# Keeping a threshold chain and a score's input in PSUM, with a second Y pair and a two-multiplication negation on POOL

## The chip, the core and the metric

The kernel runs on one core of a Trainium2 chip. The core has five engines with a queue each: TensorE (PE, whose weight loads are shown as PEld), VectorE (DVE), ScalarE (ACT), GpSimd (POOL) and SyncE (SP, which here only issues DMAs). Each queue runs in order; the engines meet through semaphores. Matmuls write PSUM, which PE, DVE and ACT reach and POOL and the DMAs do not; everything else lies in SBUF. The metric is the device time of one execution in microseconds (us), median of several runs; less is better.

## What is computed

The input x has 8 batches of 3136 rows of 256 numbers. The first half is a layer in the frequency domain with a soft threshold, the second sends 128 rows of each batch through a small network:

```python
X = np.fft.rfft(x, axis=1)
Yr = Xr @ w_r - Xi @ w_i + b_r
Yi = Xr @ w_i + Xi @ w_r + b_i
Y* = np.sign(Y*) * np.maximum(np.abs(Y*) - lam, 0.0)        # lam = 0.01, for Yr and Yi
x = np.fft.irfft(Yr + 1j * Yi, n=3136, axis=1)
scores = np.einsum('bsd,d->bs', x, w_gate)
# per batch: the 128 rows with the largest scores
h = np.maximum(x[top] @ w1, 0.0)
out[top] = x[top] + sigmoid(scores[top])[:, None] * (h @ w2)   # other rows: out = x
```

## The kernel before

The transform of length 3136 is done as 98 x 32 with matmuls. Per batch there are five stages. s1 multiplies by the 98-point table, 16 pieces of 98 x 512, and its result goes through HBM (scratch As). s2 does the 32-point half for 13 pieces g (12 of two frequency groups, one of one) into the PSUM tile px. spectral multiplies by the complex weights into the PSUM tile py, thresholds, and leaves the pair Yh, Yl. s2i does the inverse 32-point half into a PSUM tile named s, copies it to ct, takes the scalar product with w_gate for the scores, and writes ct to HBM (scratch Cs). s1i does the inverse 98-point half and writes the output. So that fp32 keeps its precision at a fast matmul format, most operands are split into a high part (a cast on ACT) and a low part (source minus high part, on DVE or POOL), and every product is three matmuls (mm3, lines 221 to 223).

One loop of about 140 steps drives all of it. In step t it emits s1 of a piece 16 steps ahead, s2 of piece t+1, spectral of piece t, s2i of piece t-1, and s1i of a piece 17 steps back; 104 steps have a spectral piece. Threads of the routing half (select, place, gather, the network) are ticked along between them; their small matmuls use the PSUM tile m. The queues are not written by hand: a scheduler that keeps the program's priorities, its pools of buffers and its own estimates of durations decides the order on each engine. A pool hands a buffer out again when the last reader of its former content is done, so a change of what reads a buffer changes waits as well.

PSUM has eight banks and all are used: four for s (s1, s2i and s1i take turns), one for px, two for py, one for m.

The lines that matter here. In spectral, line 438 adds the bias plus 0.01 to py and writes v in SBUF (DVE); line 440 makes r1 = relu(v - 0.02) on ACT; line 441 makes r1 = min(v, 0) + r1 (DVE), which is the soft threshold; line 442 splits r1 by lines 215 (Yh, ACT) and 217 (Yl = r1 - Yh, DVE). The profile names r1 as r. There is one pair Yh, Yl (YB = 1). In s2i, line 459 copies s to ct (ACT) and line 462, twice, multiplies ct by wgb and sums (DVE; the page calls it CUSTOM_DVE_ANT_0 with an accumulator read behind it). In s2, lines 420 and 421 write Xh and its negated part (ACT), line 422 writes Xl (DVE) and line 423 its negated part (POOL). Line 217 also stands for POOL's two low parts xl and cl, from SBUF only. In consts_a, lines 168 to 172 load the two weights through the buffers v and split them.

Of the kernel before, what the change touches and what calls it, by code (L numbers as in the profile page):

```python
# [10 lines left out]
F32 = mybir.dt.float32  # L11
# [5 lines left out]
AF = mybir.ActivationFunctionType  # L17
ALU = mybir.AluOpType

B, S, D = 8, 3136, 256  # L20
N1, N2 = 98, 32
NJ = 25
NF = 64
# [85 lines left out]
def fourier_moe(ctx: ExitStack, tc: tile.TileContext, x, w_r, w_i, b_r, b_i, wg, w1, w2,  # L109
                t_w1, t_w1t, t_wf, t_wq, t_g, t_gi, t_m, t_dig, outs, cap):  # L110
    nc = tc.nc
# [3 lines left out]
    pool = ctx.enter_context(tc.tile_pool(name="work", bufs=2))  # L115
# [6 lines left out]
    As, Cs, xt, xs, at, ct, av, cv, cs, ot, X, Y, Csc = [{} for _ in range(13)]  # L122

    def c_tile(shape, dt, name):
        return const.tile(shape, dt, name=name)
# [9 lines left out]
    bias = c_tile([128, 2, D], F32, "bias")  # L135
    m2l = c_tile([128, 1], F32, "m2l")
# [24 lines left out]
    def ld(out, src):  # L161
        queued(nc.sync, lambda: nc.sync.dma_start(out=out, in_=src))
# [3 lines left out]

    def consts_a():
        for src, h, l in ((w_r, wrh, wrl), (w_i, wih, wil)):
            t = pool.tile([128, 2, D], F32, name="v")
            ld(t, src.rearrange("(h p) e -> p h e", p=128))  # L170
            nc.vector.tensor_copy(h, t)
            nc.vector.tensor_tensor(out=l, in0=t, in1=h.bitcast(F32), op=ALU.subtract)
        for c, src in enumerate((b_r, b_i)):
            ld(bias[c * NF:(c + 1) * NF], src.rearrange("(o a e) -> o a e", o=1, a=1).broadcast_to([NF, 2, D]))
        nc.vector.tensor_scalar(out=bias, in0=bias, scalar1=LAM, scalar2=None, op0=ALU.add)
        nc.vector.memset(m2l, -2.0 * LAM)
# [32 lines left out]
    def pair(h_shape, tag, bufs):  # L209
        return (pool.tile(h_shape, F32R, name=tag + "h", bufs=bufs),  # L210
                pool.tile(h_shape, F32R, name=tag + "l", bufs=bufs))

    def split(src, tag, bufs, sub, track={}):
        h = pool.tile(list(src.shape), F32R, name=tag + "h", bufs=bufs)
        nc.scalar.copy(out=h, in_=src)  # L215
        l = pool.tile(list(src.shape), F32R, name=tag + "l", bufs=bufs)
        track[sub] = sub.tensor_tensor(out=l, in0=src, in1=h.bitcast(F32), op=ALU.subtract).ins  # L217
        return h, l

    def mm3(out, wh, wl, mh, ml, start=True, stop=True):  # L220
        nc.tensor.matmul(out, wh, mh, start=start, stop=False)  # L221
        nc.tensor.matmul(out, wl, mh, start=False, stop=False)  # L222
        return nc.tensor.matmul(out, wh, ml, start=False, stop=stop).ins  # L223
# [140 lines left out]
    def jview(t):  # L364
        return t[:96].rearrange("(j q) n d -> j (q n) d", q=4)

    def tail_rows(t):
        return t[96:].rearrange("q n d -> (q n) d")

    def width(g):  # L370
        return 1 if g == G - 1 else 2
# [38 lines left out]
    def s2(b, g):  # L410
        a = av.pop((b, g))
        w = width(g)
        r = a.shape[0]
        px = ps.tile([128, 2 * w, 128], F32, name="px", bufs=1)
        for p in range(w):
            for h in range(2):
                nc.tensor.matmul(px[:, 2 * p + h, :], a[:, 2 * (g % 2) * (w - 1) + p, h * 128:(h + 1) * 128],  # L417
                                 g_sb[:r, 2 * g + p, :], start=True, stop=True)
        xh, xl = pair([128, 2 * w, 3 * NF], "X", 2)
        nc.scalar.copy(out=xh[:, :, NF:], in_=px)  # L420
        nc.scalar.mul(out=xh[:, :, :NF], in_=px[:, :, NF:], mul=-1.0)  # L421
        nc.vector.tensor_tensor(out=xl[:, :, NF:], in0=px, in1=xh[:, :, NF:].bitcast(F32), op=ALU.subtract)  # L422
        nc.gpsimd.tensor_scalar(out=xl[:, :, :NF], in0=xl[:, :, 2 * NF:].bitcast(F32), scalar1=-1.0, scalar2=None, op0=ALU.mult)  # L423
        X[b, g] = xh, xl

    def spectral(b, g):
        w = width(g)
        py = ps.tile([128, w, D], F32, name="py", bufs=2)
        xh, xl = X.pop((b, g))
        for p in range(w):  # L430
            k = 0
            for sl, wh, wl in ((slice(NF, 3 * NF), wrh, wrl), (slice(0, 2 * NF), wih, wil)):
                for h in range(2):
                    mm3(py[:, p, :], xh[:, 2 * p + h, sl], xl[:, 2 * p + h, sl], wh[:, h, :], wl[:, h, :],
                        start=(k == 0), stop=(k == 3))
                    k += 1
        v = pool.tile([128, w, D], F32, name="v")
        nc.vector.tensor_tensor(out=v, in0=py, in1=bias[:, :w, :], op=ALU.add)  # L438
        r1 = pool.tile([128, w, D], F32, name="r1",bufs=1)
        nc.scalar.activation(out=r1, in_=v, func=AF.Relu, bias=m2l, scale=1.0)  # L440
        nc.vector.scalar_tensor_tensor(out=r1, in0=v, scalar=0.0, in1=r1, op0=ALU.min, op1=ALU.add)  # L441
        Y[b, g] = split(r1, "Y", YB, nc.vector)

    def s2i(b, g):
        w = width(g)
        if g == 0:
            Cs[b] = dram.tile([N1, N2, D], F32, name="Cs")
            Csc[b] = pool.tile([128, NJ], F32, name="Csc")
            nc.vector.memset(Csc[b][:, NJ - 1:], 0.0)
        if g % 2 == 0:  # L450
            ct[b] = pool.tile([128, 4, D], F32, name="ct")
        yh, yl = Y.pop((b, g))
        r = 128 if w == 2 else 64
        p = ps.tile([r, w, D], F32, name="s", bufs=4)
        for q in range(w):
            mm3(p[:, q, :], gih[:, 2 * g + q, :r], gil[:, 2 * g + q, :r], yh[:, q, :], yl[:, q, :])
        o = 2 * (g % 2)
        c = ct[b][:r, o:o + w, :]
        nc.scalar.copy(out=c, in_=p)  # L459
        for k in range(w):  # L460
            junk = pool.tile([128, D], F32, name="junk", bufs=1)
            nc.vector.tensor_tensor_reduce(out=junk[:r], in0=c[:, k, :], in1=wgb[:r], scale=1.0, scalar=0.0,  # L462
                                           op0=ALU.mult, op1=ALU.add, accum_out=Csc[b][:r, 2 * g + k:2 * g + k + 1])
        if w == 1:
            nc.sync.dma_start(out=tail_rows(Cs[b]), in_=c[:, 0, :])
        elif g % 2 == 1:
            nc.sync.dma_start(out=jview(Cs[b])[2 * g - 2:2 * g + 2].rearrange("j p d -> p j d"), in_=ct[b])

# [35 lines left out]
        if i % 2 == 1:  # L504
            nc.sync.dma_start(out=ov[b][:, 2 * i - 2:2 * i + 2, :], in_=ot[b])

    HB, YB = 2, 1
    G, U = 13, 16
    main_pe = [None]
    LEAD, LAG, XP, AP = 16, 17, 4, 2  # L510
# [69 lines left out]
    for t in range(-LEAD - XP, B * G + LAG + 1):  # L580
        if t + LEAD + XP < G:
            at_step(t + LEAD + XP, ld_x, U)
        at_step(t + LEAD + 1, split_x, U)
        at_step(t - LAG + 1, split_c, U)
        at_step(t + LEAD, s1, U)
        at_step(t + AP, ld_a, G)
        if t + LEAD + XP >= G:
            at_step(t + LEAD + XP, ld_x, U)
        at_step(t - LAG + 2, ld_c, U)
        if t == -LEAD + 7:  # L590
            consts_a()
        if t % 2 == 0 and (t + 4) // 2 in range(0, 7):
            consts_g((t + 4) // 2)
        if t % 2 and (t + 1) // 2 in range(0, 7):
            consts_gi((t + 1) // 2)
        if t == 10:
            consts_b()
        if t in range(20, 20 + 2 * (FF // 128 + 2), 2):
            consts_moe((t - 20) // 2)
        at_step(t + 1, s2, G)  # L600
        tick(threads)
        at_step(t, spectral, G)
        at_step(t - 1, s2i, G, "s2i")
        tick(threads)
        at_step(t - LAG, s1i, U, "s1i")
        if main_pe[0] is not None:
            with tc.issue_after(main_pe[0]):
                tick(ffns)
# [29 lines left out]
```

## Time and profile before

| what | us |
|---|---|
| median of 3 runs (lowest, highest) | 802.58 (802.05, 802.77) |
| the profiled execution, span of its core | 802.3 |
| PE busy in it | 745.9 (93%) |
| PEld busy | 654.1 (82%) |
| DVE busy | 616.3 (77%) |
| ACT busy | 489.5 (61%) |
| POOL busy | 427.9 (53%) |

The profile shows one execution, so durations and waits come from that one; its span is within 0.3 us of the median, and no more of its time is given than the span. PE's busy share counts matmuls whose ends are modelled and overlap, so it overstates how near PE is to its own limit; the share of weight loads, of which there is one per matmul, is the better sign of pace. An idle stretch of an engine costs only where another engine waits for it later.

### The profile page before, as it was taken

Reading aid. Unit: us, or ns where it says so; the run is one execution under the profiler, and the core shown is the slowest. Engines: PE = TensorE matmul, PEld = TensorE weight load, DVE = VectorE, ACT = ScalarE, POOL = GpSimd, SP = SyncE. Lnnn points to the kernel's source line nnn. Section 1 sums busy time; section 2 is a strip of 40 time slices with the busy share of each in tenths; the row PEclk is TensorE's granted clock in tenths of the full one; section 3 lists DMA queues with packets and bytes.
Section 4 is the critical chain, followed back from the end, with each engine's and each line's share of the span. In section 5 each row is a group of like instructions: output and inputs, shape, how many; then the busy total and the mean of one; then the engine's idle time right before and its main releaser. Section 6 shows DMA issues by size and latency. Waiting matters only on the chain.

```text
span 802.3 us, 14914 instructions
## 1 busy us (share of the span) xinstructions
PE 745.9 (93%) x5194; PEld 654.1 (82%) x5194; DVE 616.3 (77%) x1430; ACT 489.5 (61%) x970; POOL 427.9 (53%) x382
## 2 busy tenths in 40 slices
PE   6899999999999999999988899898999999899986
PEld 2389998998998899979887798777988888788756
DVE  1358877777767777778999889897689789998662
ACT  1456666778687777777666566665466465546331
POOL 1665656777676756666556655566454343444111
PEclk9589999999999999999999999998999999999999
DMA  8898676977878877777766666566464455433740
GB/s 247 284 325 271 188 251 221 291 236 243 244 223 259 253 229 230 247 239 236 219 184 210 205 192 208 191 205 183 154 193 157 147 158 152 145 105 105 251 149 27
DMA packets 86825, 165.58 MB, mean 206 GB/s; under 512 B 6589, under 2 KB 59358, under 8 KB 86750
## 3 DMA queue, kind: packets, MB, share of 16 engines
q1 hardware_dynamic: 83070, 154.58, 62.1%
q0 software_dynamic: 3568, 10.02, 3.9%
q8 instruction: 41, 0.67, 0.3%
q14 instruction: 34, 0.28, 0.1%
q10 hardware_dynamic: 112, 0.04, 0.0%
HBM read 86.56 MB, written 78.12 MB: 205 GB/s over the span
## 4 chain that ended last, share of the span: by engine, by line
PE 52%; DVE 25%; DMA 7%; ACT 7%; issue 7%; POOL 1%; SPq 0%; POOLq 0%; ACTq 0%; DVEq 0%
PE py L221 7%; PE py L223 7%; PE py L222 7%; PE px L417 6%; PE s L223 6%; PE s L221 5%; PE s L222 5%; DVE Yl L217 4%; DVE junk L462 4%; DVE r L441 3%; DVE Xl L422 2%; DVE v L438 2%; ACT Yh L215 2%; DVE c L242 2%; DMA av<-As 2%
## 5 line engine op out<-in xcount | busy, mean ns | idle before, releaser
L217 POOL TENSOR_TENSOR cl<-cv,ch 98x512 fp32r<-98x512 f32 x112 | 150.5, 1345 | 159.0 <-ACT ch L215 147.7
L217 POOL TENSOR_TENSOR xl<-xt,xh 98x512 fp32r<-98x512 f32 x112 | 153.4, 1372 | 70.4 <-ACT xh L215 65.4
L459 ACT COPY ct<-s 128x512 f32<-128x512 f32 (+1 forms) x104 | 59.3, 570 | 143.2 <-PE s L223 140.0
L462 DVE CUSTOM_DVE_ANT_0 junk<-ct,wgb 128x256 f32<-128x256 f32 (+1 forms) x200 | 113.4, 567 | 31.1 <-ACT ct L459 28.1
L217 DVE TENSOR_TENSOR Yl<-r,Yh 128x512 fp32r<-128x512 f32 (+1 forms) x104 | 105.6, 1015 | 29.2 <-ACT Yh L215 26.4
L221 PE MATMUL py<-wrh,Xh 128*128 128x256 f32 x400 | 123.0, 307 | 0.7 <-ACT Xh L420 0.7
L423 POOL TENSOR_SCALAR Xl<-Xl 128x256 fp32r<-128x256 f32 (+1 forms) x104 | 92.4, 889 | 54.2 <-DVE Xl L422 33.0
L417 PEld LDWEIGHTS px<-g_sb,av 128*128 128x128 f32 (+1 forms) x800 | 105.7, 194 | 19.1 <-PE s L223 4.0
L222 PE MATMUL py<-wih,Xl 128*128 128x256 f32 x400 | 114.0, 285 | 1.4 <-POOL Xl L423 1.4
L223 PE MATMUL py<-wil,Xh 128*128 128x256 f32 x400 | 114.5, 286 | 0.0
L222 PE MATMUL py<-wrh,Xl 128*128 128x256 f32 x400 | 114.3, 286 | 0.0
L221 PE MATMUL py<-wih,Xh 128*128 128x256 f32 x400 | 114.2, 285 | 0.0
L223 PE MATMUL py<-wrl,Xh 128*128 128x256 f32 x400 | 114.0, 285 | 0.0
L417 PE MATMUL px<-g_sb,av 128*128 128x128 f32 (+1 forms) x800 | 109.5, 279 | 4.0 <-DVE Xl L422 2.5
L440 ACT ACTIVATE r<-v,m2l 128x512 f32<-128x512 f32 (+1 forms) x104 | 73.7, 708 | 38.1 <-DVE v L438 35.4
L422 DVE TENSOR_TENSOR Xl<-px,Xh 128x512 fp32r<-128x512 f32 (+1 forms) x104 | 69.0, 664 | 24.9 <-ACT Xh L421 20.3
L438 DVE TENSOR_TENSOR v<-py,bias 128x512 f32<-128x512 f32 (+1 forms) x104 | 68.9, 663 | 24.2 <-PE py L223 23.4
L441 DVE SCALAR_TENSOR_TENSOR r<-v,r 128x512 f32<-128x512 f32 (+1 forms) x104 | 82.1, 790 | 4.1 <-ACT r L440 3.7
L215 ACT CAST Yh<-r 128x512 fp32r<-128x512 f32 (+1 forms) x104 | 62.9, 605 | 34.2 <-DVE r L441 33.8
L221 PEld LDWEIGHTS py<-wrh,Xh 128*128 128x128 f32 x400 | 76.8, 192 | 6.0 <-issue 3.7
L222 PEld LDWEIGHTS py<-wih,Xl 128*128 128x128 f32 x400 | 76.6, 191 | 2.4 <-POOL Xl L423 1.6
L222 PEld LDWEIGHTS py<-wrh,Xl 128*128 128x128 f32 x400 | 77.0, 193 | 1.5 <-issue 1.2
(139 smaller groups left out, 1802.4 us busy)
## 6 DMA issues: line engine op xcount, KB each, us to landing
av<-As SPq DMA_DIRECT2D x48, 512.0 KB
Cs<-ct SPq DMA_DIRECT2D x48, 512.0 KB
xt<-in_x SPq DMA_DIRECT2D x60, 392.0 KB
out<-ot SPq DMA_DIRECT2D x60, 392.0 KB
cv<-Cs SPq DMA_DIRECT2D x59, 392.0 KB
As<-at SPq DMA_DIRECT2D x53, 392.0 KB
As<-at POOLq DMA_DIRECT2D x11, 392.0 KB, 7.0
gip<-t_gi POOLq DMA_DIRECT2D x6, 512.0 KB, 6.7
```

Of the source, the lines that this page charges most:

```text
L215: nc.scalar.copy(out=h, in_=src)
L217: track[sub] = sub.tensor_tensor(out=l, in0=src, in1=h.bitcast(F32), op=ALU.subtract).ins
L221: nc.tensor.matmul(out, wh, mh, start=start, stop=False)
L222: nc.tensor.matmul(out, wl, mh, start=False, stop=False)
L223: return nc.tensor.matmul(out, wh, ml, start=False, stop=stop).ins
L417: nc.tensor.matmul(px[:, 2 * p + h, :], a[:, 2 * (g % 2) * (w - 1) + p, h * 128:(h + 1) * 128], g_sb[:r, 2 * g + p, :], start=True, stop=True)
L422: nc.vector.tensor_tensor(out=xl[:, :, NF:], in0=px, in1=xh[:, :, NF:].bitcast(F32), op=ALU.subtract)
L423: nc.gpsimd.tensor_scalar(out=xl[:, :, :NF], in0=xl[:, :, 2 * NF:].bitcast(F32), scalar1=-1.0, scalar2=None, op0=ALU.mult)
L438: nc.vector.tensor_tensor(out=v, in0=py, in1=bias[:, :w, :], op=ALU.add)
L440: nc.scalar.activation(out=r1, in_=v, func=AF.Relu, bias=m2l, scale=1.0)
L441: nc.vector.scalar_tensor_tensor(out=r1, in0=v, scalar=0.0, in1=r1, op0=ALU.min, op1=ALU.add)
L462: nc.vector.tensor_tensor_reduce(out=junk[:r], in0=c[:, k, :], in1=wgb[:r], scale=1.0, scalar=0.0, op0=ALU.mult, op1=ALU.add, accum_out=Cs ...
```

## The change

```diff
@@ consts_a
-            t = pool.tile([128, 2, D], F32, name="v")
+            t = pool.tile([128, 2, D], F32, name="r1", bufs=1)
@@ s2
-        nc.gpsimd.tensor_scalar(out=xl[:, :, :NF], in0=xl[:, :, 2 * NF:].bitcast(F32), scalar1=-1.0, scalar2=None, op0=ALU.mult)
+        nc.gpsimd.tensor_scalar(out=xl[:, :, :NF], in0=xl[:, :, 2 * NF:].bitcast(F32), scalar1=-1.0, scalar2=1.0, op0=ALU.mult, op1=ALU.mult)
@@ spectral
-        v = pool.tile([128, w, D], F32, name="v")
-        nc.vector.tensor_tensor(out=v, in0=py, in1=bias[:, :w, :], op=ALU.add)
-        r1 = pool.tile([128, w, D], F32, name="r1",bufs=1)
-        nc.scalar.activation(out=r1, in_=v, func=AF.Relu, bias=m2l, scale=1.0)
-        nc.vector.scalar_tensor_tensor(out=r1, in0=v, scalar=0.0, in1=r1, op0=ALU.min, op1=ALU.add)
-        Y[b, g] = split(r1, "Y", YB, nc.vector)
+        nc.vector.tensor_tensor(out=py, in0=py, in1=bias[:, :w, :], op=ALU.add)
+        r1 = pool.tile([128, w, D], F32, name="r1", bufs=1)
+        nc.scalar.activation(out=r1, in_=py, func=AF.Relu, bias=m2l, scale=1.0)
+        nc.vector.scalar_tensor_tensor(out=py, in0=py, scalar=0.0, in1=r1, op0=ALU.min, op1=ALU.add)
+        Y[b, g] = split(py, "Y", YB, nc.vector)
@@ s2i
         nc.scalar.copy(out=c, in_=p)
+        c = p
...
-            nc.sync.dma_start(out=tail_rows(Cs[b]), in_=c[:, 0, :])
+            nc.sync.dma_start(out=tail_rows(Cs[b]), in_=ct[b][:r, o, :])
@@ top level
-    HB, YB = 2, 1
+    HB, YB = 2, 2
```

The bias is added to py in place, the threshold's second step writes py again, and both halves of the split read py, so that v is gone and the py bank stays in use until Yl is written. The score's multiply-and-sum reads the PSUM tile s in place of ct; ct is still written, for HBM. The negation on POOL carries a second multiplication, by 1. There are two pairs Yh, Yl. The weights in consts_a pass through the one buffer r1 in place of two buffers v.

The first place where instructions move is the start, on SP's queue: the loads of the two weights (in_w_r, in_w_i), of the biases, and of three tiles of x for batch 1. Before:

```order
L162 DMA v<-in_w_r 128x2x256
L162 DMA v<-in_w_i 128x2x256
L162 DMA bias<-in_b_r 64x2x256 [waits DMAHW3_49]
L162 DMA bias<-in_b_i 64x2x256 [waits DMAHW4_49]
L162 DMA xt<-in_x 98x1024 [waits DMAHW5_49,PE_49]
```

and now:

```order
L162 DMA r_149<-in_w_r 128x2x256
L162 DMA r_153<-in_w_i 128x2x256 [waits DMAHW1_49,DVE_49]
L162 DMA bias<-in_b_r 64x2x256 [waits DMAHW3_49]
L162 DMA bias<-in_b_i 64x2x256 [waits DMAHW4_49]
L162 DMA xt<-in_x 98x1024 [waits DMAHW5_49,PE_49]
```

The order is the same, but the second weight's load now waits for DVE, which must have split the first weight, and everything behind it on SP waits with it.

The second is DVE's queue at the same place; at is the tile in which s1 of batch 0 is copied out, wrh to wil the split weights. Before:

```order
L171 CAST wrh<-v 128x512 [waits DMAHW1_49]
L172 TENSOR_TENSOR wrl<-v,wrh 128x512 [waits DVE_49]
L171 CAST wih<-v 128x512 [waits DMAHW2_49]
L396 COPY at<-s 98x512 [waits DMASW4_49,PE_49,Activation_49]
L172 TENSOR_TENSOR wil<-v,wih 128x512 [waits DVE_49]
```

and now:

```order
L171 CAST wrh<-r_149 128x512 [waits DMAHW1_49]
L172 TENSOR_TENSOR wrl<-r_149,wrh 128x512 [waits DVE_49]
L396 COPY at<-s 98x512 [waits DMASW4_49,PE_49,Activation_49]
L396 COPY at<-s 98x512 [waits DMASW5_49,PE_49,Activation_49]
L171 CAST wih<-r_153 128x512 [waits DMAHW2_49]
L172 TENSOR_TENSOR wil<-r_153,wih 128x512 [waits DVE_49]
```

The two copies of at now stand ahead of the second weight's split.

The third is one step in the middle of the program on DVE: Yl of one piece, Xl of the next, and the threshold and score instructions of the step. Before:

```order
L217 TENSOR_TENSOR Yl<-r_3929,Yh 128x512 [waits PE_49,Activation_49]
L422 TENSOR_TENSOR Xl<-px,Xh 128x4x128 [waits PE_49,Activation_49,Pool_49]
L438 TENSOR_TENSOR v<-py,bias 128x512 [waits PE_49]
L462 ISA junk,Csc<-ct,wgb 128x256 [waits Activation_49]
L462 ISA Csc 128x1
L462 ISA junk,Csc<-ct,wgb 128x256 [waits DVE_49]
L441 SCALAR_TENSOR_TENSOR r_4013<-v,r_4013 128x512 [waits Activation_49]
```

and now:

```order
L217 TENSOR_TENSOR Yl<-py,Yh 128x512 [waits Activation_49]
L422 TENSOR_TENSOR Xl<-px,Xh 128x4x128 [waits PE_49,Activation_49,Pool_49]
L437 TENSOR_TENSOR py<-py,bias 128x512 [waits PE_49]
L462 ISA junk,Csc<-s,wgb 128x256 [waits DVE_49,Activation_49]
L462 ISA Csc 128x1
L462 ISA junk,Csc<-s,wgb 128x256 [waits DVE_49]
L440 SCALAR_TENSOR_TENSOR py<-py,r_3967 128x512 [waits Activation_49]
```

The order within the step is the same; what differs is that each of these instructions now has one operand in PSUM and at most one in SBUF among its inputs, and that Yl no longer waits for PE to give the Y pair back. Around the routing threads' instructions some neighbours change places.

## Rows read from the trace of the kernel before

**Rows 1.** The head of the profile's page: the span, and for each engine busy us, share of the span and instructions.

```profile
span 802.3 us, 14914 instructions
PE 745.9 (93%) x5194; PEld 654.1 (82%) x5194; DVE 616.3 (77%) x1430; ACT 489.5 (61%) x970; POOL 427.9 (53%) x382
```

**Rows 2.** Busy time by stretch of the program, all engines: the stretch, its length, then per engine busy us and instructions, then the granted share of TensorE's full clock, the DMA engines' busy share, GB/s.

```profile
40.00:400.00 360.00, 350.84 (x2568) 320.60 (x2567) 273.97 (x523) 256.51 (x513) 233.91 (x202) 0.99 0.79 245
80.00:120.00 40.00, 39.89 (x308) 37.29 (x306) 32.28 (x67) 25.66 (x53) 23.63 (x21) 1.00 0.68 219
400.00:560.00 160.00, 141.78 (x967) 125.42 (x966) 145.04 (x318) 101.25 (x201) 92.31 (x79) 0.97 0.64 195
560.00:720.00 160.00, 150.43 (x1123) 137.51 (x1122) 137.62 (x392) 88.14 (x174) 67.36 (x59) 0.99 0.49 153
```

**Rows 3.** Groups of DVE instructions by line and shape: count | busy us, mean ns of one | idle before them and what ended it.

```profile
L462 DVE CUSTOM_DVE_ANT_0 junk<-ct,wgb 128x256 f32<-128x256 f32 x192 | 109.5, 570 | 30.8 <-ACT ct L459 28.1
L217 DVE TENSOR_TENSOR Yl<-r,Yh 128x512 fp32r<-128x512 f32 x96 | 99.2, 1034 | 28.7 <-ACT Yh L215 26.2
L441 DVE SCALAR_TENSOR_TENSOR r<-v,r 128x512 f32<-128x512 f32 x96 | 76.1, 792 | 3.4 <-ACT r L440 3.1
L422 DVE TENSOR_TENSOR Xl<-px,Xh 128x512 fp32r<-128x512 f32 x96 | 65.7, 684 | 23.0 <-ACT Xh L421 20.0 <-POOL cl L217 1.4 <-issue 0.2
L438 DVE TENSOR_TENSOR v<-py,bias 128x256 f32<-128x256 f32 x8 | 3.3, 412 | 0.0
```

**Rows 4.** The timeline of one step in the steady part, from which rows are left out: start us, duration us, engine, line and operation, out<-in, shapes, in brackets the idle time before it and what ended it.

```profile
299.47 1.29 POOL L217 TENSOR_TENSOR cl<-cv,ch 98x512 fp32r<-98x512 f32 x1 [1.40 <-PE px L417]
...
300.00 1.32 DVE L217 TENSOR_TENSOR Yl<-r,Yh 128x512 fp32r<-128x512 f32 x1
...
302.32 0.69 DVE L438 TENSOR_TENSOR v<-py,bias 128x512 f32<-128x512 f32 x1 [0.40 <-PE py L223]
...
302.59 0.85 POOL L423 TENSOR_SCALAR Xl<-Xl 128x256 fp32r<-128x256 f32 x1
...
303.66 0.43 DVE L462 CUSTOM_DVE_ANT_0 junk<-ct,wgb 128x256 f32<-128x256 f32 x1 [0.64 <-ACT ct L459]
...
304.48 0.68 DVE L441 SCALAR_TENSOR_TENSOR r<-v,r 128x512 f32<-128x512 f32 x1
...
304.93 0.39 PE L221 MATMUL s<-xh,w1p 98*98 98x512 f32 x1
...
305.85 0.69 DVE L217 TENSOR_TENSOR Yl<-r,Yh 128x512 fp32r<-128x512 f32 x1 [0.69 <-ACT Yh L215]
...
306.42 0.36 PE L221 MATMUL py<-wrh,Xh 128*128 128x256 f32 x1
```

**Rows 5.** Busy time of DVE's instructions of line 217 alone (Yl), by stretch: the stretch, its length, busy us and instructions, granted clock, DMA share, GB/s.

```profile
40.00:400.00 360.00, 56.21 (x58) 0.99 0.79 245
400.00:560.00 160.00, 26.25 (x21) 0.97 0.64 195
560.00:720.00 160.00, 18.59 (x21) 0.99 0.49 153
```

**Rows 6.** The same for line 441, the threshold's second step.

```profile
40.00:400.00 360.00, 49.56 (x58) 0.99 0.79 245
400.00:560.00 160.00, 14.96 (x21) 0.97 0.64 195
560.00:720.00 160.00, 15.14 (x21) 0.99 0.49 153
```

**Rows 7.** The same for line 462, the score; its count holds the accumulator reads too, one for each multiply-and-sum.

```profile
40.00:400.00 360.00, 67.21 (x220) 0.99 0.79 245
400.00:560.00 160.00, 22.42 (x80) 0.97 0.64 195
560.00:720.00 160.00, 20.44 (x82) 0.99 0.49 153
```

**Rows 8.** Waits of PE's matmuls in the stretch from 40 to 400 us: engine and line, whom it waited for, us in total, times, longest.

```profile
PE s L221 <- ACT Yh L215: 3.8, 3, 1.5
PE s L223 <- DVE Yl L217: 2.4, 9, 0.5
```

**Rows 9.** The same from 400 to 560 us; hl, ok are small tiles of the routing threads and their network.

```profile
PE s L223 <- DVE Yl L217: 4.4, 7, 1.4
...
PE m L277 <- DVE hl L350: 2.9, 1, 2.9
...
PE m L471 <- DVE ok L262: 2.8, 1, 2.8
```

**Rows 10.** The timeline of the start on SP (SPq: DMA issues), DVE and ACT, rows left out.

```profile
12.62 0.49 SPq L162 DMA_DIRECT2D v<-in_w_i  x1
...
14.62 0.55 SPq L162 DMA_DIRECT2D xt<-in_x  x1
...
24.03 0.69 DVE L172 TENSOR_TENSOR wrl<-v,wrh 128x512 fp32r<-128x512 f32 x1
...
27.75 0.62 ACT L215 CAST xh<-xt 98x512 fp32r<-98x512 f32 x1
```

**Rows 11.** Groups of POOL's instructions of line 423 (the negation), by shape.

```profile
L423 POOL TENSOR_SCALAR Xl<-Xl 128x256 fp32r<-128x256 f32 x96 | 87.8, 914 | 45.9 <-DVE Xl L422 27.5 <-DVE w L265 4.5 <-DVE ok L262 4.2
...
L423 POOL TENSOR_SCALAR Xl<-Xl 128x128 fp32r<-128x128 f32 x8 | 4.6, 580 | 8.2 <-DVE Xl L422 5.5 <-PE s L223 2.7
```

## The prediction, made before the changed kernel ran

> **What bounds the kernel now.** I read the head of the page first: PE is busy for 93% of an 802.3 us span, DVE for 77% [rows 1]. Taken alone this says PE, but the mean hides two kinds of stretch, so I read busy time by stretch next [rows 2]. There is one weight load per matmul, so the busy share of loads is a pace. From 80 to 120 us it is 37.29 of 40 (0.932), which I take as PE's own pace, with nothing late. From 40 to 400 us it is 320.60 of 360 (0.891): PE works almost at that pace, and DVE has 86 us idle of 360. From 400 to 560 us it is 125.42 of 160 (0.784), while DVE is busy for 145.04 of 160: there DVE sets the end, because the routing threads put their small instructions on it. From 560 to 720 us it is 137.51 (0.859) with DVE at 137.62, a mixture. At 0.932 the loads of the three stretches would take 344, 134.6 and 147.5 us, so the room above PE's own pace is 16, 25 and 12.5 us. No change to DVE can bring back more than about 53 us.
>
> Then the groups on DVE [rows 3]. Xl takes 684 ns for 512 elements with one operand in PSUM and one in SBUF; Yl does the same subtraction on two SBUF operands and takes 1034 ns; the threshold's second step takes 792 and the score's product 570 for 256 elements. The timeline of one step tells why [rows 4]: with POOL idle Yl takes 0.69, the threshold step 0.68 and the score 0.43 us; the Yl that starts at 300.00 while POOL is in the middle of a low part from SBUF (299.47, 1.29 long) takes 1.32. DVE instructions with two SBUF operands wait for POOL; Xl, which reads PSUM, keeps its 684 as a mean over 96 although POOL is busy half the time.
>
> **The change, part by part.** *Yl, threshold, score.* All three are left with one SBUF operand. If they then run as Xl does, the excess over their undisturbed times goes. By stretch [rows 5 to 7], against 0.69, 0.685 and 0.43 us (the accumulator read overlaps the product, so a product with its read is 0.43):
> 40 to 400: 56.21 - 58 x 0.69 = 16.2; 49.56 - 58 x 0.685 = 9.8; 67.21 - 110 x 0.43 = 19.9; sum 46 us.
> 400 to 560: 11.8 + 0.6 + 5.2 = 17.6 us.
> 560 to 720: 4.1 + 0.8 + 2.8 = 7.7 us.
> Most of DVE's relief thus falls where DVE is not the bound. What it is worth in each stretch:
>
> In 40 to 400 us, the end is set by PE, and only waits on the Y pair go: PE waited 3.8 us for Yh and 2.4 us for Yl [rows 8]. An undisturbed step has Yl done at 306.54, when the next spectral starts at 306.42 [rows 4], and the product that needs it comes behind the matmuls of that spectral, so these waits occur only where DVE was held up. I take 8 us, near the 6.2 of the waits and far from the 16 of the room, because a late Yl also delays loads a little without a named wait.
>
> In 400 to 560 us, 17.6 us of DVE's work go and PE has room for 25. DVE's queue is in order, so the routing instructions for which PE waits (hl 2.9, ok 2.8 us) come earlier just as Yl does (4.4) [rows 9]. I take two thirds, 12 us: DVE also has 15 us idle there, and excess that stands ahead of such an idle time buys nothing. In 560 to 720 us I take 4.5 of 7.7 by the same reasoning. What is late next is PE itself, then the round trips of the routing threads between PE and DVE.
>
> *The clock.* The granted clock averages 0.97 in 400 to 560 us [rows 2], 0.03 below full, so some 10 us ran at the lower of the two levels (1.2 in place of 2.4 GHz), at a cost of about 5 us. Shorter stalls may spare part of it; I take 2.
>
> *Writes into PSUM.* The bias step and the threshold step now write PSUM from DVE, 208 instructions; no row shows such a write. The bounds: a 512-element instruction has 684 - 412 = 272 ns for 256 elements, 1.06 ns an element, and about 140 ns fixed [rows 3]; at best the fixed part vanishes (-0.14 us), at worst an element that is read and written in one bank takes twice as long (+0.54 us). I take 0, since the nearest row, Xl with its read from PSUM, shows no surcharge over 0.69 for SBUF alone. Here a rule speaks against the change. The Trainium skill, page "Perfetto Trace Analysis", section "Optimizing Scalar/DVE Operations", gives DVE a fixed cost of about 60 ns per instruction on SBUF and 125 on PSUM. For reads the trace disagrees: 684 against 690. An estimate from that page would add 65 ns to five instructions of each step, 0.33 us, or 14 us of DVE's time over the 42 steps between 400 and 720 us.
>
> *Banks held longer.* py is now busy until Yl is written, about 4.2 us after its matmuls end instead of 0.7. Two banks and a step of 6.2 to 7.6 us (360 us for 58 pieces, 160 for 21) [rows 5] leave room: the spectral that takes this bank again is the one after that at 306.42, some 6 us behind this Yl. An s bank is free only after the score's second product: in the step shown it is done when the threshold step starts, at 304.48, and the fourth tile behind it starts at 304.93 [rows 4]. That is tight only in steps with two pieces each of s1 and s1i; I take 1 us lost in all, where DVE is behind.
>
> *The start.* The load of w_i was issued at 12.62 and the first x tile of batch 1 behind it at 14.62; now w_i waits until wrl is done, at 24.03 + 0.69 = 24.72 by the old times, and the x tile goes out at some 26.5. It was first read at 27.75 [rows 10]. A tile of 98 x 1024 fp32 numbers is 0.4 MB, 1.6 us at the 245 GB/s of [rows 2] and more beside other traffic, so it lands between 28 and 31 and up to 3 us are lost; on the other side the writes of batch 0 have the DMA engines to themselves, which brings DVE's copies, the split and the release forward. Bounds -2 (a gain) to +3; I take 1 us lost.
>
> *POOL's negation.* 914 ns for 256 elements and 580 for 128 [rows 11]: 334 ns per 128, so a second pass over 256 would add 0.67 us, and a faster path could save as much. It stands at 302.59 to 303.44 for a spectral that starts at 306.42 [rows 4]; 3 us of slack cover either, and POOL is at 53% [rows 1]. Uncovered it would be 0.67 us a step. *Second Y pair.* Yh waits for the previous product only where Yl was late already. *ACT* reads py in place of SBUF. I put all three at nothing.
>
> **Sum.** 8 + 12 + 4.5 + 2 - 1 - 1 = 24.5 us. The span is 802.3 and the median 802.6; 802.6 - 24.5 = **778 us**. Its own range, with each term's bounds, is 768 to 786.
>
> **The rivals.** *DVE stops being a bound at all.* The routing round trips speed up with everything else and PE keeps 0.932 nearly throughout: 10 + 25 + 12.5 less 1 is about 46, so 756 us. For it: one queue feeds all those waits. Against it: DVE would still be busy for 127 of some 135 us there.
>
> *The saving is given back.* PSUM operands cost something, or the waits in the routing threads are round trips that a shorter Yl does not touch; then only named waits on the pair go: 6 + 5 + 2 and nothing for the clock, 789 us. For it: a good half of PE's named waits from 400 us on are for hl, ok and their like [rows 9]. The page named above would have about this time.
>
> *Slower.* Place: the two in-place writes of each step on DVE. At +0.54 us each DVE gains 22.7 us of work in 400 to 560 (42 writes) against 17.6 saved, and 22.7 against 7.7 in 560 to 720, where DVE has 22 us idle, so about half of the 15 counts: +5 + 7, and 2 for the banks, less 4 that the first stretch keeps, 812 us. It decides from about 0.4 us a write on (25.3 us saved over 84 writes is 0.3; the first stretch carries it further). Against it: nothing in the rows hints at a slow bank.
>
> *It doesn't do what it says.* POOL holds DVE up through the one SBUF operand as well, and only the names move: about 802 us. Against it: Xl's 684.
>
> **How the numbers follow.** Forecast 0.55; DVE no bound 0.12; given back 0.20; slower 0.09; no effect 0.04. The range takes in the given-back case and the upper half of the no-bound case: 757 to 795 us, which leaves out about 0.18. A measurement here tells some 0.2%, 1.6 us, from no change: faster 0.87, same 0.04, slower 0.09.
>
> **What would show it.** Right: Yl and the threshold step near 690 ns, the score's product near 430, with no long ones; DVE busy near 540 us; loads above 0.84 in 400 to 560; PE's waits for Yl nearly gone. Wrong: bias or threshold step well over 700 ns (the write), new waits of PE on line 462 or of spectral's first matmul on Yl (the banks), the whole steady part shifted by more than 3 us (the start), or PE waiting for POOL's line 423.

## The result, and the profile after

The changed kernel takes **773.6 us** (median of 4 runs, 771.3 to 774.7) against 802.7 (802.1 to 804.9) for the kernel before on the same chip: ratio 0.9625, 95% interval 0.960 to 0.965. The forecast was 778, inside a range of 757 to 795. The profiled execution took 774.0 us, its span is 772.2.

The head of the page of the kernel after (the span; per engine busy us, share, instructions), and the first line of its chain of waits:

```profile
span 772.2 us, 14915 instructions
PE 729.9 (95%) x5194; PEld 646.9 (84%) x5194; DVE 542.7 (70%) x1430; ACT 478.0 (62%) x970; POOL 362.0 (47%) x382
PE 67%; DVE 15%; DMA 7%; issue 5%; ACT 4%; POOL 1%; SPq 0%; POOLq 0%; ACTq 0%; DVEq 0%
```

Beside [rows 1]: 74 us of DVE's work and 66 of POOL's are gone, and so are 30 us of the span; less than half of what DVE was spared reached the end. The groups of DVE and of POOL (count | busy us, mean ns | idle before, and what ended it):

```profile
L462 DVE CUSTOM_DVE_ANT_0 junk<-s,wgb 128x256 f32<-128x256 f32 x192 | 81.0, 422 | 34.8 <-ACT ct L458 31.9
L437 DVE TENSOR_TENSOR py<-py,bias 128x512 f32<-128x512 f32 x96 | 66.8, 695 | 39.9 <-PE py L223 39.8
L440 DVE SCALAR_TENSOR_TENSOR py<-py,r 128x512 f32<-128x512 f32 x96 | 66.7, 695 | 7.3 <-ACT r L439 6.6 <-issue 0.3
L217 DVE TENSOR_TENSOR Yl<-py,Yh 128x512 fp32r<-128x512 f32 x96 | 66.0, 688 | 37.4 <-ACT Yh L215 37.2
L423 POOL TENSOR_SCALAR Xl<-Xl 128x256 fp32r<-128x256 f32 x96 | 39.0, 407 | 41.0 <-DVE Xl L422 24.9 <-DVE f L239 4.6 <-DVE w L265 4.3
```

Yl went from 1034 to 688 ns, the threshold's second step from 792 to 695, the score's product from 570 to 422 [rows 3]. The bias step and the threshold step, which now write PSUM in place, take 695 ns, where the bias step took 684 with its output in SBUF: a 512-element write into PSUM costs DVE about 11 ns more than one into SBUF, not 540. POOL's negation, with a second multiplication, fell from 914 [rows 11] to 407 ns.

Busy time by stretch, the same stretches as [rows 2]:

```profile
40.00:400.00 360.00, 355.29 (x2618) 326.18 (x2618) 236.24 (x537) 255.07 (x525) 202.01 (x210) 1.00 0.79 251
400.00:560.00 160.00, 153.88 (x1102) 138.04 (x1100) 135.65 (x351) 105.83 (x214) 83.56 (x83) 0.99 0.67 212
560.00:720.00 160.00, 154.08 (x1153) 139.89 (x1152) 135.25 (x423) 92.62 (x189) 57.20 (x60) 1.00 0.50 156
```

The second figure after the length is PE's loads: from 400 to 560 us they rose from 125.42 to 138.04, from 560 to 720 from 137.51 to 139.89. PE's waits in 40 to 400 us, and then in 400 to 560, beside [rows 8, 9]:

```profile
PE s L221 <- ACT Yh L215: 1.5, 1, 1.5
...
PE s L221 <- DVE Csc L462: 0.4, 1, 0.4
PE s L223 <- DVE Yl L217: 0.3, 1, 0.3
```

```profile
PE s L223 <- DVE Yl L217: 1.9, 4, 0.8
PE m L252 <- DVE n L247: 1.8, 1, 1.8
PE m L307 <- DVE hot L302: 1.3, 2, 0.8
PE s L221 <- DVE Csc L462: 0.8, 1, 0.8
```

In 40 to 400 us the waits for the Y pair went from 6.2 to 1.8 us. In 400 to 560 those for Yl went from 4.4 to 1.9, the 2.9 for hl are gone and of the 2.8 for ok 0.2 are left; a wait for n grew from 0.6 to 1.8. The new wait for Csc is the s bank, now held until the score has read it: 1.2 us in all.

Where along the program the time was gained is read from the start of one and the same instruction in both traces: the first product of the spectral of pieces 9, 59, 80 and 104 of 104 (the timeline of PE, rows left out; before, then after).

```profile
85.19 0.37 PE L221 MATMUL py<-wrh,Xh 128*128 128x256 f32 x1
...
395.82 0.36 PE L221 MATMUL py<-wrh,Xh 128*128 128x256 f32 x1
...
557.33 0.58 PE L221 MATMUL py<-wrh,Xh 128*128 128x256 f32 x1
...
733.78 0.28 PE L221 MATMUL py<-wrh,Xh 128*128 128x256 f32 x1
```

```profile
90.06 0.37 PE L221 MATMUL py<-wrh,Xh 128*128 128x256 f32 x1
...
390.42 0.37 PE L221 MATMUL py<-wrh,Xh 128*128 128x256 f32 x1
...
535.38 0.39 PE L221 MATMUL py<-wrh,Xh 128*128 128x256 f32 x1
...
701.67 0.28 PE L221 MATMUL py<-wrh,Xh 128*128 128x256 f32 x1
```

The new kernel stands at -4.9 us at piece 9, +5.4 at 59, +22.0 at 80, +32.1 at 104, and +30.1 at the end of the span. So the start lost 4.9, the stretches gained 10.3, 16.6 and 10.1, and the tail gave 2.0 back.

The start's loss has a name. SP's queue after the change, PE's longest wait, and PE's first product on a tile of x, before and then after:

```profile
12.79 0.41 SPq L162 DMA_DIRECT2D r<-in_w_r  x1
21.98 0.39 SPq L162 DMA_DIRECT2D r<-in_w_i  x1
...
24.62 3.61 SPq L162 DMA_DIRECT2D xt<-in_x  x3
```

```profile
PE s L221 <- ACT xh L215: 9.8, 2, 9.5
```

```profile
28.43 0.47 PE L221 MATMUL s<-xh,w1p 98*98 98x512 f32 x1 [0.80 <-DVE at L396]
```

```profile
32.97 0.74 PE L221 MATMUL s<-xh,w1p 98*98 98x512 f32 x1 [9.55 <-ACT xh L215]
```

w_i goes out at 21.98 in place of 12.62 [rows 10], because it now waits for DVE's split of w_r in the one r1 buffer; the x tiles behind it go out at 24.62 in place of 14.62, PE stands for 9.5 us, and its first product on x comes 4.5 us later than before.

### The profile page after: what moved, and what is told of

Read it like the earlier page. It is cut to its first block, busy times and chain, and to the rows that moved or that the text cites. A ratio compares the mean times of both kernels' runs of the same rounds, so it can differ in the third digit from the quotient of the medians.

```text
span 772.2 us, 14915 instructions
## 1 busy us (share of the span) xinstructions
PE 729.9 (95%) x5194; PEld 646.9 (84%) x5194; DVE 542.7 (70%) x1430; ACT 478.0 (62%) x970; POOL 362.0 (47%) x382
## 4 chain that ended last, share of the span: by engine, by line
PE 67%; DVE 15%; DMA 7%; issue 5%; ACT 4%; POOL 1%; SPq 0%; POOLq 0%; ACTq 0%; DVEq 0%
PE py L221 9%; PE py L223 9%; PE py L222 9%; PE px L417 9%; PE s L221 8%; PE s L223 8%; PE s L222 7%; DMA As<-at 2%; DVE Xl L422 2%; PE m L346 2%; DVE Yl L217 2%; DVE c L242 1%; DVE w L265 1%; DVE junk L462 1%; DVE py L437 1%
## 5 line engine op out<-in xcount | busy, mean ns | idle before, releaser
L217 POOL TENSOR_TENSOR cl<-cv,ch 98x512 fp32r<-98x512 f32 x112 | 144.5, 1292 | 205.6 <-ACT ch L215 141.9
L217 POOL TENSOR_TENSOR xl<-xt,xh 98x512 fp32r<-98x512 f32 x112 | 144.3, 1292 | 82.3 <-ACT xh L215 74.4
L462 DVE CUSTOM_DVE_ANT_0 junk<-s,wgb 128x256 f32<-128x256 f32 (+1 forms) x200 | 84.3, 421 | 35.0 <-ACT ct L458 31.9
L437 DVE TENSOR_TENSOR py<-py,bias 128x512 f32<-128x512 f32 (+1 forms) x104 | 70.1, 674 | 40.4 <-PE py L223 40.3
L217 DVE TENSOR_TENSOR Yl<-py,Yh 128x512 fp32r<-128x512 f32 (+1 forms) x104 | 69.4, 667 | 37.7 <-ACT Yh L215 37.4
L439 ACT ACTIVATE r<-py,m2l 128x512 f32<-128x512 f32 (+1 forms) x104 | 70.2, 675 | 26.3 <-DVE py L437 21.6
L215 ACT CAST xh<-xt 98x512 fp32r<-98x512 f32 x112 | 71.8, 645 | 12.9 <-DMA xt<-in_x 8.9
L221 PEld LDWEIGHTS py<-wih,Xh 128*128 128x128 f32 x400 | 75.7, 189 | 0.9 <-issue 0.9
L440 DVE SCALAR_TENSOR_TENSOR py<-py,r 128x512 f32<-128x512 f32 (+1 forms) x104 | 70.2, 675 | 8.8 <-ACT r L439 8.0
L223 PEld LDWEIGHTS py<-wrl,Xh 128*128 128x128 f32 x400 | 75.8, 190 | 0.4 <-issue 0.3
```

Of the source, the lines that this page charges most:

```text
L437: nc.vector.tensor_tensor(out=py, in0=py, in1=bias[:, :w, :], op=ALU.add)
L439: nc.scalar.activation(out=r1, in_=py, func=AF.Relu, bias=m2l, scale=1.0)
L440: nc.vector.scalar_tensor_tensor(out=py, in0=py, scalar=0.0, in1=r1, op0=ALU.min, op1=ALU.add)
```

## The experiments

Times are medians of 6 executions, but for the change itself (4, as above). The twelve kernels were measured in three groups of four, in which the kernel before had 803.8, 803.0 and 800.8 us. The leads in the table are worked out as above, from the start of the spectral's first product for a piece in each trace (before minus run; "end" from the spans). They come from one execution each: those of score_only, chain_only and neg_only took 4.0, 5.4 and 4.5 us more than their medians, so their leads at the end are 4 to 5 us short of what the medians give, and the gains below are taken from the medians. Two traces of the changed kernel (the change, after_again) agree within 0.5 us.

```
                 us      ratio (95%)            lead at piece 9    59     80    104    end
the change      773.6  0.9625 (0.960-0.965)          -4.9    5.4   22.0   32.1   30.1
score_only      779.9  0.9704 (0.967-0.973)          -2.6    5.9   19.1   22.5   20.2
chain_only      773.7  0.9623 (0.959-0.966)          -4.0    3.2   22.1   30.0   25.0
neg_only        792.3  0.9859 (0.983-0.989)          -1.0   -0.9    7.2    9.1    7.3
after_start     771.3  0.9588 (0.955-0.962)           1.5   10.8   25.6   35.7   31.4
early_half      794.2  0.9896 (0.985-0.994)           1.0   10.0   11.8   13.1    8.5
late_half       777.9  0.9695 (0.966-0.973)          -0.3    1.1   17.9   28.0   26.1
after_neg1      769.5  0.9591 (0.955-0.963)          -3.8    5.6   25.5   35.7   32.2
after_y1        772.2  0.9627 (0.960-0.966)          -2.0    7.8   24.1   34.2   32.6
before_nolow    749.1  0.9333 (0.929-0.938)          -4.6    9.3   37.3   54.7   54.9
after_nolow     752.5  0.9370 (0.932-0.942)          -3.8    9.7   37.6   55.1   51.1
start_y1        771.0  0.9612 (0.956-0.967)           0.0    9.1   26.0   36.1   33.3
after_again     772.8  0.9630 (0.958-0.968)          -4.4    5.6   22.0   32.2   30.6
```

**Is it POOL's hold on DVE?** The kernel before, with POOL's two wide subtractions of a step cut to 8 columns. PE takes the high part where it took the low one, so the results lack the low part:

```diff
+        if sub is nc.gpsimd:
+            l = pool.tile([N1, 8], F32R, name=tag + "l", bufs=bufs)
+            track[sub] = sub.tensor_tensor(out=l, in0=src[:, 0, :8], in1=h[:, 0, :8].bitcast(F32), op=ALU.subtract).ins
+            return h, h
```

> The kernel before with POOL's low parts of x and c left out: its two subtractions of 98 x 512 per step are cut to 8 columns, and PE takes the high part once more in place of the low one, so PE has the same matmuls and the results lack the low part. POOL's negation and all of DVE's work stay as before, with two SBUF operands. Theory (DVE's instructions with several SBUF operands are not slow themselves, they are held up while POOL works from SBUF): Yl falls from 1034 to below 780 ns, the score's product from 570 to below 460, the threshold step from 792 to below 720, and the time to that of the changed kernel or below it, since this kernel has no loss at the start and its routing is spared too: 765 us (759 to 771). Rival (two SBUF operands cost this much by themselves): Yl above 900 ns and 790 us or more.

Measured: 749.1 us, 10 below the range expected. Its DVE groups:

```profile
L466 DVE CUSTOM_DVE_ANT_0 junk<-ct,wgb 128x256 f32<-128x256 f32 x192 | 81.3, 424 | 41.8 <-ACT ct L463 39.0
L221 DVE TENSOR_TENSOR Yl<-r,Yh 128x512 fp32r<-128x512 f32 x96 | 66.3, 690 | 28.0 <-ACT Yh L215 26.4
...
L445 DVE SCALAR_TENSOR_TENSOR r<-v,r 128x512 f32<-128x512 f32 x96 | 65.8, 686 | 3.7 <-ACT r L444 3.6
...
L246 DVE TENSOR_TENSOR c<-scores,f 98x384 bf16<-98x384 f32 x15 | 8.8, 584 | 0.4
...
L269 DVE SCALAR_TENSOR_TENSOR w<-d,w 98x4 uint32<-98x4 uint32 x16 | 2.6, 161 | 0.3
```

With two SBUF operands as before, Yl takes 690, the threshold step 686 and the product 424 ns. The excess on these instructions was POOL's subtractions, and a kernel without them is 52 us faster; the change brings 29. The 52 is not DVE's relief alone, since PE no longer waits for POOL's low part xl either; before, its named waits for xl were 1.2 us of matmuls and 4.1 of weight loads. The trace of the kernel before says the same of Yl without any change: counted one by one, the 73 of its 96 wide instructions that overlap a low part on POOL take 1143 ns in the mean, the 21 that overlap neither a low part nor a negation 687. The Trainium skill, page "SBUF — State Buffer", section "SBUF: two separate sides", says that a DVE instruction with two SBUF inputs and a GpSimd instruction that reads SBUF exclude each other for a whole instruction. The trace agrees: 1034 against 690 ns.

**What is left of it after the change?** The same lines in the changed kernel.

> The changed kernel with the same cut of POOL's low parts. Theory (what is left of POOL's hold on DVE is in the routing's instructions, which still take SBUF operands): the wide instructions of the chain stay at 690 and 420 ns, the routing's compare c of 98 x 384 falls from 832 to below 650 ns, and the time falls by some 5 to 10 us below the changed kernel's: 766 us (762 to 769), with the same loss at the start. Rival (POOL no longer costs the changed kernel anything): 771 to 775.

Measured: 752.5 us, 20 below the changed kernel, twice the largest gain expected. The wide instructions do not move (422, 694 and 689 ns), the routing's do. Two of them in the changed kernel, then with its low parts cut:

```profile
L242 DVE TENSOR_TENSOR c<-scores,f 98x384 bf16<-98x384 f32 x15 | 12.5, 831 | 0.4
L265 DVE SCALAR_TENSOR_TENSOR w<-d,w 98x4 uint32<-98x4 uint32 x16 | 12.4, 778 | 0.3
```

```profile
L246 DVE TENSOR_TENSOR c<-scores,f 98x384 bf16<-98x384 f32 x15 | 8.6, 575 | 0.4
L269 DVE SCALAR_TENSOR_TENSOR w<-d,w 98x4 uint32<-98x4 uint32 x16 | 2.5, 158 | 0.3
```

An instruction on 4 numbers per partition takes 778 ns where it takes 158 with the low parts cut: it waits for POOL's instruction, however small it is itself. Up to piece 104 the two cut kernels stand level (54.7 and 55.1), and the one with PSUM operands is no faster in the median: with POOL's low parts gone they bring nothing that shows.

**Which part brings it?** Three runs, each the kernel before with one group of the diff's lines: the score, the chain (py in place of v and r1, the constants through r1), the negation.

```diff
 score_only
+        c = p
...
 chain_only
+        nc.vector.tensor_tensor(out=py, in0=py, in1=bias[:, :w, :], op=ALU.add)
...
+        nc.vector.scalar_tensor_tensor(out=py, in0=py, scalar=0.0, in1=r1, op0=ALU.min, op1=ALU.add)
...
 neg_only
+        nc.gpsimd.tensor_scalar(..., scalar1=-1.0, scalar2=1.0, op0=ALU.mult, op1=ALU.mult)
```

> The kernel before with one part of the change: the score's product reads the s bank in PSUM in place of its SBUF copy. Theory (an SBUF operand that DVE shares with a second SBUF operand is what POOL holds up): the product falls from 570 to about 425 ns, Yl and the threshold step stay near 1034 and 792 ns, and of the 29 us some 6 to 10 come, 794 us, most of it from 400 us on, where DVE sets the end. Rival (the gain belongs to the Y chain alone, the score is always hidden): the product falls as well, but the time stays within 2 us of 802.7. Rival (the bank s is held longer and PE waits for it): PE shows waits on line 462 of over 3 us and the time is above 800.

> The change without its score part, its two multiplications on POOL and its second Y pair: threshold chain in place in PSUM, constants through the one r1 buffer. Theory: Yl and the threshold step near 690 ns, the product of the score still near 550, POOL's negation 914; the start loses the same 5 us; the rest of the gain is somewhat over half of 35, so about 785 us (780 to 790). Rival (gain is mainly the score's relief or POOL's faster negation): 795 or more.

> The kernel before with POOL's negation as two multiplications and nothing else. Theory: the negation falls from 914 to about 410 ns, POOL is busy some 50 us less, but the negation is hidden (3 us of slack in a step), so the time is 802.7 within 3 us; Yl may fall somewhat below 1034 if POOL holds DVE up during the negation as well. Rival (POOL's shorter work is what freed DVE): Yl falls below 900 and the time below 792.

Measured: 779.9, 773.7 and 792.3 us. The single steps save 24, 30 and 11.5 us, the whole 29: the parts do not add up, and each of the three gains lies outside what was expected of it. The score's 24 were put at 6 to 10, and in its trace it gains 8.5 us between pieces 9 and 59 already, where the prediction had given the score nothing. Its two products stand ahead of the threshold step in DVE's queue [rows 4], so a late product can make Yl late; that this is the way is argued, not shown. The chain alone, put at 780 to 790, is level with the whole change. The negation alone was expected to give nothing, and Yl did stay at 1037; yet in its trace it won 8.1 us between pieces 59 and 80. The timelines of the two show how; DVE and POOL before, then DVE and POOL with the short negation:

```profile
499.70 1.77 DVE L441 SCALAR_TENSOR_TENSOR r<-v,r 128x512 f32<-128x512 f32 x1
...
499.61 1.31 POOL L217 TENSOR_TENSOR cl<-cv,ch 98x512 fp32r<-98x512 f32 x1 [0.82 <-ACT ch L215]
```

```profile
499.12 0.69 DVE L441 SCALAR_TENSOR_TENSOR r<-v,r 128x512 f32<-128x512 f32 x1
...
496.94 1.27 POOL L217 TENSOR_TENSOR xl<-xt,xh 98x512 fp32r<-98x512 f32 x1
499.49 1.47 POOL L217 TENSOR_TENSOR cl<-cv,ch 98x512 fp32r<-98x512 f32 x1 [1.27 <-ACT ch L215]
```

Up to here PE runs within 0.2 us of the same place in both traces. Before, the threshold step starts 0.09 us behind a low part and takes 1.77 us. With the short negation POOL's xl begins earlier, a small mask instruction takes 0.57 in place of 1.01 us, and the same step starts 0.37 us ahead of that low part and takes 0.69. The next spectral then starts at 504.7 in place of 506.4. This collision is 1.6 of the 8.1 us; 2.9 more are PE's wait for hl just ahead of piece 80, which is gone there (one of 1.4 us comes after that piece). Behind such waits the clock counts too: from 506 to 516 and from 550 to 570 us the granted clock averages 0.83 before and 1.00 with the short negation, and 0.17 of these 30 us is 5 us at most of the 10 that the negation gains between pieces 59 and 104. So where DVE sets the end, one met or missed collision moves what stands behind it, and a shorter wait can spare a stretch at the lower of the clock's two levels.

**The side parts, taken back from the changed kernel.** One multiplication (after_neg1); one Y pair (after_y1):

```diff
+        scalar1=-1.0, scalar2=None, op0=ALU.mult)
...
+    HB, YB = 2, 1
```

> The changed kernel with POOL's negation as one multiplication again. Theory (with the chain and the score in PSUM, POOL no longer holds DVE up, and the negation itself is hidden): negation back at some 880 ns, time the changed kernel's 773.6 within 2 us. Rival (the 11 us that the negation alone brought came through POOL's own results): 778 or more, with PE waiting for Xl of line 423.

> The changed kernel with one Y pair. Theory (Yh waits for the previous product only where Yl was late already): 773.6 within 2 us, PE's waits for Yh and Yl below 6 us in all. Rival (the second pair is what lets PE run ahead): 777 or more, with ACT's Yh waiting for PE line 223.

Measured: 769.5 and 772.2 us, neither slower than the change; the first is 2 us below the range expected, with an interval that meets that of the change. With the chain and the score in PSUM the negation at 852 ns costs nothing that can be measured, and the second Y pair brings nothing.

**Do the stretches add up?** All three edits for batches 0 to 3, or for 4 to 7 alone (as shown here), start and Y pair as before:

```diff
...
+        new = b >= 4
+        v = py if new else pool.tile([128, w, D], F32, name="v")
...
+        y = py if new else r1
...
+        c = p if new else c
```

> The kernel before, with threshold chain, score and negation changed for batches 0 to 3 alone (their last spectral starts at about 356 us); start and Y pair as before. Theory (each stretch gives its own part, as the prediction's terms assume): up to 400 us some 8 to 11 us are gained and kept, from there on it goes as before: 792 us (789 to 795). Rival (the 10 us that even the negation alone brought are no relief of DVE but a matter of how the late waits fall, and any shift brings them): 782. Rival (the early gain is taken back later because the late stretch waits for something else): 800 or more.

> The kernel before, with threshold chain, score and negation changed for batches 4 to 7 alone; start and Y pair as before. Theory (each stretch gives its own part): nothing up to 356 us, then what the full change gained from there on, about 26 to 28 us without its loss at the start: 776 us (773 to 780); loads above 0.84 in 400 to 560, one or no stretch of half clock there. Rival (in the late stretch only some 10 us depend on DVE's operands): 792.

Measured: 794.2 and 777.9 us, gains of 8.8 and 25.1, as the first theory of each said. Their sum is 34, and less the start's 5 it is the 29 of the change. What the first half gains is kept up to piece 104; in its trace 4.6 us go in the tail, where the granted clock averages 0.91 against 0.97 before. This also answers the rival that any shift of the late steps brings what the negation brought: early_half comes to piece 59 10.0 us early, its waits for hl and ok are still 2.9 and 2.8 us, and it gains only 1.8 more up to piece 80.

**The start.** The constants through the two ct buffers, which are free until the first inverse stage; with two Y pairs, with one, and the change itself beside the latter:

```diff
-            t = pool.tile([128, 2, D], F32, name="r1", bufs=1)
+            t = pool.tile([128, 4, D], F32, name="ct")[:, :2, :]
```

> The changed kernel with the constants of the start loaded through the two ct buffers, which nothing uses before the first inverse stage, in place of the one r1 buffer: w_i's load no longer waits for DVE's split of w_r. Theory: PE's wait of 9.5 us for xh at the start falls below 3, the first spectrals start some 4 to 5 us earlier and nothing later takes it back: 769 us (767.5 to 770.5). Rival (PE's early start collides with something else, or the later waits take it back): 772 or more.

> The changed kernel with both of its side parts taken back: one Y pair, and the start's constants through the two ct buffers. Theory: no wait of PE for xh above 3 us at the start, the second pair gives nothing, 768 us (766 to 770.5). Rival (the second pair makes up for something once the start is earlier): 772 or more.

> The changed kernel once more, beside the three others of this group: 773.5 us (771.5 to 775.5), and more than 2 us above the version with one Y pair and the start's constants through ct.

Measured: 771.3, 771.0 and 772.8 us. PE's wait for xh is gone (0.6 us and none), and piece 9 starts 4 to 6 us earlier; at piece 104 some 4 us are left, at the end 1 to 3. The gain of about 2 us is inside the intervals, so it is not shown, and the 4 to 5 us that were expected at the end did not come; after_again lies 1.7 above start_y1, where more than 2 were expected. A lead at piece 9 is not the loads' alone: score_only and before_nolow keep the two buffers and stand 2.6 and 4.6 us behind there, with a granted clock from 28 to 90 us of 0.86 and 0.81 against 0.89 before. After the change it is 0.88, so its 4.9 us are not the clock's. Part of it goes in the tail. PE's wait there, after the change and with the early start:

```profile
PE s L500 <- DMA xt<-Cs: 1.1, 1, 1.1
```

```profile
PE s L500 <- DMA xt<-Cs: 1.7, 1, 1.7
```

Neither the kernel before nor start_y1 has such a wait of 0.5 us or more there. The granted clock also averages 0.95 in the 72.8 us behind piece 104 with the early start, against 0.98 in the 70.5 after the change. Why it fell there stays open.

## Why the prediction was right, step by step

**The mechanism** was right: two SBUF operands on DVE are held up by POOL, and one is not. It is shown by the cut of POOL's low parts, not by the durations of the change alone. DVE's busy time was to be near 540 us (542.7), Yl and the threshold step near 690 (688, 695), the product near 430 (422), loads above 0.84 in 400 to 560 (0.863). The bound on any gain from DVE, 53 us, stands beside the 52 of the kernel whose low parts are cut.

**The sizes** were off by more than the total shows:

- 40 to 400 us, +8: 10.3. Two thirds of the room, where named waits held 6.2. The attribution to the Y pair alone was too narrow, since the score's edit by itself brings 8.5 there.
- 400 to 560 us, +12, and clock +2: 16.6 together (pieces 59 to 80). The granted clock rose from 0.97 to 0.99 of 160 us and from 0.99 to 1.00 in the next stretch, which is worth 3 to 5 us at most, so the clock may have been under-sized. What it really gave is open: after_again has 1.00 in both stretches and the same leads.
- 560 to 720 us, +4.5: 10.1 (pieces 80 to 104), the largest miss, and the step that failed is the two thirds "by the same reasoning". Scaling DVE's spared time by two thirds assumed that an excess costs at most itself. As the collision at 499.70 shows, a held-up instruction stands in an in-order queue and delays what PE and the routing wait for, and behind PE's idle time the clock fell. In the trace before, from 546.0 to 556.4 us PE was busy for 8.27 of 10.4, in the 6.9 us after that the granted clock averages 0.51, and the product at 557.33 takes 0.58 us where the same product takes 0.36 at piece 59. How the 10.1 divide between such delays and the clock is not shown.
- The start, -1, bounds -2 to +3 lost: 4.9 lost at piece 9. The step that failed is the transfer: the tile was to go out "at some 26.5" and to land between 28 and 31, 1.6 us and more after its issue. It went out at 24.62, earlier than taken, but ACT waited for it until 32.30, 7.7 us after its issue, and PE's first product on it started at 32.97 in place of 28.43. The load of w_i, issued at 21.98, was likewise in use only at 28.00; what held these loads is not shown. The steady part was thus shifted by more than the 3 us that the prediction had named as a sign of being wrong about the start. What it costs at the end is smaller, about 2 us and not resolved.
- Banks held longer, -1: 1.2 us of waits, right. The tail, not in the sum: -2.0.
- PSUM writes at 0: 11 ns each, 208 of them 2.3 us of DVE's time, right. The rule of the Trainium skill's page "Perfetto Trace Analysis", section "Optimizing Scalar/DVE Operations" (60 ns on SBUF, 125 on PSUM) is not seen: 695 ns in PSUM, 686 to 690 in SBUF with POOL's low parts cut. The cost of PSUM operands behind the rival at 789 falls with it, and so does the slower case at 812, which needed 0.4 us a write.
- POOL's negation, the second Y pair, ACT at nothing: right for the first two beside the other edits, and ACT's part was not tried by itself. But "3 us of slack cover either" failed as a general step: in the kernel before, the shorter negation alone brings 11.5 us. PE's wait for it was 1.4 us before; for one step the trace shows that the gain came through where POOL's next subtraction falls on DVE.
- "DVE stops being a bound", 756: no. PE keeps 0.863 and 0.874 of the two late stretches in loads. What is left is above all the routing's own instructions under POOL's hold: cutting the low parts gives 20 us more, and loads of 145.69 of the 160 us from 400 to 560 (0.911). That too takes POOL's own lateness with it, 0.2 us of named waits of matmuls and 2.3 of loads. The forecast spoke of round trips there; much of them is this.

The gains were put too low by 2.3, 2.6 and 5.6 us, together 10.5; the start's loss (3.9 more than taken) and the tail (2.0) took more than half of that back, and the miss of the median is 4.4 us. That the terms' errors went against each other is luck; the mechanism is not.

## What to carry to other kernels

Look for DVE instructions that take longer than others of their form, and see in the timeline whether POOL is reading SBUF at that moment; one operand in PSUM frees them, and so does a quiet POOL, and small instructions are held up as well as wide ones. Here the parts that relieve the same in-order queue did not add up, and the two halves of the program did: price such a change per stretch, and try its parts alone, since here the chain by itself gave all of it. When a buffer is merged to make room, follow the loads that are queued behind the one that now waits.

## What the runs showed of the hardware that was not expected

- POOL's tensor_scalar on 128 x 256 fp32r numbers takes 914 ns with one multiplication and 407 with two (852 against 407 with the chain and score in PSUM; 890 against 428 with POOL's low parts cut). Which path makes the longer form the faster one, no run here tells.
- A DVE instruction on 98 x 4 numbers takes 778 ns in the mean beside POOL's subtractions and 158 without them.
- POOL gains by it as well: its two groups of low parts of 98 x 512 took 1372 and 1345 ns in the mean and both take 1292 after the change.
- DVE writes PSUM in place, on the bank that it reads, in 695 ns for 512 numbers, against 684 with the output in SBUF.
